# Linear attention with a gated MLP: the first v loads issued by ACT's queue, and twelve zero products fewer ahead of the first product with q

## The chip, the cores and the metric

The kernel runs on one core of one Trainium2 chip. The metric is the device time of one launch in microseconds (us), the median over runs. Engines are named as the profile names them: PE (matrix products), PEld (its weight loads), DVE, ACT and POOL (elementwise work), SP (which here only issues DMAs). ACT can issue DMAs too.

## The reference

```
kv  = einsum('bhsd,bhse->bhde', k, v)            # batch 8, heads 8, seq 576, head_dim 64
out = einsum('bhsd,bhde->bhse', q, kv)
x   = out / sqrt(mean(out*out, -1) + 1e-6) * g_norm     # heads joined: 8 x 576 x 512
h   = gelu_tanh(x @ w_in)                        # 512 -> 1024, split into u and v
v_n = (v - mean(v)) / sqrt(var(v) + 1e-6) * g_ln
v_s = einsum('ts,bsd->btd', w_sg, v_n) + b_sg[None, :, None]
y   = x + (u * v_s) @ w_out
```

## The kernel before

All eight batches run in one stream. The order of the work is written out by hand: `ORDER` is a list of words, each a step of one batch and index (`K01` is step K of batch 0, index 1), and each engine executes its instructions in the order in which the list issues them. The steps that matter here:

- `k` (load_kv, L288-296) issues the loads of one chunk of 128 tokens of k and of v; batch 0 has five (`k00` to `k04`, the last of 64 tokens), 256 KB a load for the first four and 128 KB for the last. Both go through SP's queue, k then v.
- `K` (kv, L298-313) multiplies k and v of a chunk on PE (tile `pkv`); `K04` closes batch 0. `c` (kv_high, L322-325) copies the sum out on ACT (tile `kvf`).
- `q` loads a pair of heads of q; `o` (L345-353) multiplies it with `kvf` on PE into tile `po`, eight times a batch, into the four PSUM banks "ps". `f` (o_scale) writes x from `po` with the factor g (on DVE in `f00v`), `e` (o_square) writes the squares on ACT, `s` sums them on PE.
- `N` (warm, L182-185) is two 128x512 products of a tile of zeros, whose result nobody reads. They go to the same four banks.
- `D`, `A`, `E`, `B`, `L`, `C`, `F`, `I` load a piece of w_in, w_out or w_sg and turn it from 64-bit words into two floats: A on ACT (L233), E, B and L on DVE (L241, L237, L245), C on POOL (L248), F on ACT (L259), I on POOL or DVE (L277). `F21` makes the factor g on DVE (L269).

`constants()` runs ahead of the list. Its ACT part is one small gelu, which brings an ACT_TABLE_LOAD with it.

A DMA's completion is told by one of eight semaphores, DMAHW0 to DMAHW7, shared by all DMA queues and given out in turn, so that a DMA is issued only when the earlier one on its semaphore has landed.

Of the kernel before, what the change touches and what calls it, by code (L numbers as in the profile page):

```python
# [19 lines left out]
NC = S // P  # L20
# [25 lines left out]
    t05 N31 j00 c10 j01 N32 c11 D17 j02 A04 o10 j03 j04 o11 e10 B04 k21 N33 A05 E04 N34 j05 e11 N35 B05 f10a T00 s10
    E05 f11a o12 D07 T01 T02 o13 D23 f12a T03 M04 T04 M06 e12 M02 f13v D20 M07 e13 o14 x07v o15 L05 e14 M01 F16 s11
    f14v C05 x01v e15 o16 f15v F17 M00 I16p s12 x06v f16a K20 x00v e16 I17v X00 o17 D18 M05 Y00p x02v M03 D19 f17a
    D08 x05v e17 N36 D09 x03v F20 s13 k22 x04v N37 t10 N38 k23 L04 X01 I21p N39 t11 N40 X02 N41 F18 N42 C04 N43 Y01v
    F19 m0 t12 F04 I19v F05 t13 q20 X03 I05v K21 t14 A06 Y02v Y03p t15 U00 k24 I18v k30 j10 h20 E06 q21 j11 I04v U02  # L50
    u00 j12 n00 A07 j13 n01 j14 U03 E07 u02 j15 B07 r10 n02 L07 K22 u03 n03 U06 C07 h21 k31 B06 c20 c21 r11 F07 U07
    d21 L06 u06 I07v C06 U01 u07 d20 A08 I20v F06 K30 l10 u01 r12 l11 l12 U04 l13 I06v m1 k32 E08 B08 A09 k33 V00
    n10 u04 L08 E09 C08 B09 F08 D10 n11 n12 L09 V01 n13 C09 I08v F09 D11 x10p x11v a00 I09p V02 b00 r13 a01 i20v p00
    i21v q22 y00 q23 K31 b01 z00 o20 k34 w00 p01 o21 e20 V03 k40 e21 a02 y01 b02 x13p z01 h22 w01 U05 p02 i22v a03
    x12p y02 q30 V04 u05 X10 X11 Y10v X12 Y11p b03 z02 K32 Y12v a04 k41 p03 X13 w02 Y13p V10 b04 A10 y03 p04 E10 z03
    V11 B10 L10 y04 C10 w03 z04 D12 F10 w04 S00 A11 I10v E11 S01 a10 g00 b10 G00 B11 H00 p10 S02 L11 J00 C11 g01 y10
    G01 F11 D13 S03 g02 I11p H01 J01 G02 A12 S04 g03 B12 G03 H02 E12 S05 H03 J02 g04 L12 G04 J03 P00 C12 H04 g05 J04
    G05 F12 D14 P01 Q00 I12v A13 S06 E13 Q01 B13 L13 C13 S07 g06 F13 D15 G06 I13v V12 A14 g07 z10 E14 G07 B14 w10
    L14 A15 U15 C14 E15 F14 B15 V13 f20a L15 I14v u15 C15 f21a a11 F15 b11 I15p P03 p11 a12 b12 P02 y11 p12 Q03 z11
    U16 Q02 H05 w11 H06 H07 J05 o22 a13 J06 o23 e22 b13 U12 u16 h23 f22v p13 J07 f23a P06 i23p y13 u12 e23 P07 q31  # L60
    Q06 y12 O06 z12 P05 Q07 z13 w12 O07 w13 P04 Q05 O05 o24 Q04 o25 e24 O04 U14 e25 h30 f24a i30p U13 u14 f25a q32
    o26 u13 o27 f26v e26 U11 h31 c30 i31p c31 d30 U17 u11 d31 f27a q33 e27 o30 u17 o31 f30v s20 h32 f31a i32p K40
    t20 e30 t21 e31 o32 k42 o33 t22 e32 f32v U10 k43 h33 f33v q40 e33 i33p t23 o34 u10 o35 e34 S10 q41 e35 t24 t25
    j20 j21 j22 S11 g10 j23 G10 j24 h40 K41 j25 H10 i40p g11 J10 S12 k44 G11 k50 r20 H11 S13 g12 q42 J11 G12 S14 H12
    g13 J12 G13 S15 H13 g14 r21 J13 G14 r22 P11 H14 g15 J14 G15 P12 Q11 l20 l21 l22 l23 S16 m2 Q12 n20 n21 n22 S17
    n23 g16 x21p x20v P10 G16 g17 X20 r23 G17 X21 Y20v P13 Y21p Q10 K42 Q13 H15 H16 J15 k51 H17 J16 J17 P17 P16 Q17
    O17 x23v x22p P15 Q16 O16 X22 P14 Q15 f34a Y22v O15 f35a X23 o36 Q14 o37 Y23p e36 f36v O14 V20 h41 f37v c40 i41p
    c41 d40 e37 d41 q43 s30 a20 b20 K50 t30 p20 U26 k52 t31 t32 y20 k53 t33 z20 V21 t34 u26 w20 t35 j30 j31 j32 j33
    V22 a21 j34 j35 b21 r30 p21 V23 y21 a22 z21 b22 r31 w21 p22 r32 K51 a23 y22 U23 b23 z22 k54 k60 w22 p23 U21 l30
    u23 l31 l32 l33 y23 m3 U22 z23 n30 n31 n32 x30p u21 w23 o40 u22 o41 e40 x31p U25 h42 f40v e41 n33 f41a V24 r33  # L70
    i42v u25 q50 o42 a24 o43 f42a K52 b24 h43 U20 k61 f43v p24 e42 e43 i43p y24 o44 u20 o45 e44 U24 x33p e45 q51
    x32v h50 z24 U27 i50v u24 w24 S20 q52 u27 X30 X31 Y30v S21 X32 g20 X33 Y31v G20 S22 g21 Y32p H20 J20 S23 Y33p
    g22 G22 V30 g23 G21 G23 H21 H22 J21 H23 J22 S24 a30 J23 b30 p30 P21 g24 G24 y30 P23 H24 Q21 J24 P20 Q23 S25 Q20
    V31 g25 G25 P22 a31 b31 S26 Q22 H25 p31 J25 y31 S27 g26 G26 H26 V32 g27 z30 J26 G27 z31 w30 H27 J27 P27 w31 a32
    b32 U35 Q27 p32 O27 y32 P26 z32 u35 w32 f44a U36 Q26 f45a O26 U32 u36 o46 u32 P24 f46v e46 U31 Q24 O24 P25 u31
    o47 Q25 U33 h51 f47v O25 c50 i51v c51 U37 e47 d50 q53 u33 d51 o50 u37 o51 f50a s40 f51v h52 K60 t40 e50 i52v e51
    o52 t41 q60 o53 t42 k62 f52a t43 V33 t44 f53a k63 t45 h53 j40 j41 e52 i53p j42 e53 o54 a33 o55 q61 j43 U34 e54
    b33 h60 j44 p33 e55 j45 U30 r40 u34 i60p y33 K61 u30 z33 k64 w33 S30 k70 r41 S31 g30 G30 r42 H30 S32 g31 q62 J30
    G31 S33 H31 g32 J31 G32 l40 S34 H32 l41 l42 l43 g33 m4 J32 G33 S35 n40 H33 x40v n41 X40 x41v K62 Y40p n42 X41
    r43 S36 k71 Y41v S37 n43 g34 J33 G34 g35 P31 g36 G35 H34 J34 G36 g37 P33 Q31 G37 x43v P32 x42v Q33 X42 P30 X43  # L80
    Q32 Y42p Y43p V40 Q30 H35 H36 J35 H37 J36 J37 P34 a40 b40 P35 Q34 p40 O34 y40 P36 z40 Q35 O35 w40 f54a f55v U41
    Q36 O36 o56 u41 o57 f56v e56 P37 h61 f57a i61v c60 U47 Q37 c61 e57 d60 O37 d61 q63 s50 u47 K70 t50 t51 t52 U46
    t53 k72 t54 t55 k73 j50 j51 U43 u46 j52 j53 j54 j55 V41 u43 r50 K71 r51 a41 b41 V42 r52 p41 k74 y41 z41 V43 a42
    l50 l51 l52 l53 w41 m5 b42 U40 n50 p42 a43 n51 n52 n53 x50p b43 V44 u40 x51v p43 y42 r53 z42 y43 w42 z43 K72 a44
    w43 U45 b44 U42 p44 u45 y44 z44 o60 o61 x53p U44 f60a w44 h62 x52p u42 S40 u44 i62v X50 X51 S41 Y50p X52 Y51v
    q70 e60 e61 f61a S42 Y52p X53 g40 g41 S43 g42 Y53p G42 V50 G40 G41 H40 J40 H41 g43 V51 H42 J41 a50 G43 J42 H43
    b50 o62 J43 a51 p50 P41 f62v e62 b51 P43 y50 p51 Q41 y51 P40 Q43 P42 Q40 o63 Q42 o64 f63a S44 h63 e63 i63v e64
    S45 q71 g44 G44 H44 o65 g45 S46 e65 J44 G45 h70 i70p H45 S47 J45 q72 g46 V52 G46 g47 z50 z51 w50 G47 H46 w51 H47
    U55 J46 a52 J47 b52 P46 u55 p52 y52 P45 Q46 z52 O46 w52 U56 Q45 O45 f64v P47 u56 f65v o66 Q47 U51 e66 O47 f66a
    P44 u51 U52 Q44 O44 V53 u52 o67 a53 U57 f67a b53 h71 p53 U53 c70 u57 d70 i71p c71 y53 e67 s60 u53 q73 d71 z53  # L90
    U54 t60 w53 t61 o70 t62 u54 t63 o71 f70a t64 U50 t65 h72 j60 j61 f71a i72v e70 S50 u50 j62 e71 j63 j64 j65 o72
    r60 g50 o73 f72a S51 G50 f73v h73 H50 i73v e72 J50 S52 e73 r61 g51 G51 r62 o74 H51 g52 o75 e74 J51 S53 G52 e75
    H52 l60 l61 J52 S54 l62 l63 g53 m6 G53 S55 n60 H53 g54 x60p x61v S56 G54 X60 J53 r63 X61 Y60p H54 P51 g55 J54
    Y61p P52 g56 Q51 n61 G56 n62 P53 G55 Q52 n63 S57 x63v x62p Q53 P50 X62 g57 G57 X63 Y62p Y63v V60 H55 H56 Q50 H57
    J55 J56 J57 P55 a60 b60 P54 Q55 p60 O55 y60 P56 z60 Q54 O54 w60 f74a P57 Q56 f75a O56 o76 Q57 o77 e76 f76v O57
    U66 f77a e77 s70 u66 U61 t70 t71 t72 t73 t74 U65 t75 u61 j70 j71 j72 U63 j73 u65 j74 j75 r70 V61 u63 r71 V62 a61
    r72 b61 p61 V63 y61 a62 l70 z61 l71 l72 l73 w61 m7 b62 U60 a63 n70 p62 n71 n72 n73 x70p b63 V64 u60 y62 x71p z62
    w62 U67 p63 r73 a64 b64 U62 y63 u67 p64 z63 y64 U64 u62 w63 z64 u64 w64 S60 X70 x72p X71 x73v S61 X72 Y70v Y71p
    X73 S62 g60 g61 G60 G61 H60 S63 g62 Y72p H61 Y73v V70 G62 J60 H62 J61 J62 V71 g63 a70 G63 b70 H63 p70 J63 P61
# [573 lines left out]
```

## Time and profile before

| | us |
|---|---|
| median of 3 runs | 529.02 (528.95 to 529.67) |
| the profiled execution, its own time | 528.13 |
| its span (first to last instruction) | 526.3 |
| PE busy in the span | 516.1 (98%) |

The profile is of one execution. Its span is 1.83 us shorter than its own time, which is launch and end. Times in the views count from the span's start.

### The profile page before, as it was taken

How to read it: one execution, taken by the hardware profiler on the slowest of the kernel's cores; microseconds unless marked ns; L12 is line 12 of the kernel's file. 1: busy time of each engine (PE TensorE's matmuls, PEld its weight loads, DVE VectorE, ACT ScalarE, POOL GpSimd, SP SyncE). 2: the span in 40 equal slices, each digit the busy share in tenths (PEclk: the TensorE clock that was granted, in tenths of full speed). 3: DMA queues.
4: the chain of work that ended last, by engine and by line, in shares of the span. 5: the costliest groups of instructions: out<-in, count | busy, mean ns of one | idle time of the engine just before them, and what ended most of it. 6: DMA issues, size and time to landing. Idle time of an engine off the chain costs nothing.

```text
span 526.3 us, 10121 instructions
## 1 busy us (share of the span) xinstructions
PE 516.1 (98%) x4032; PEld 476.2 (90%) x4032; DVE 313.5 (60%) x656; ACT 200.4 (38%) x449; POOL 189.3 (36%) x215
## 2 busy tenths in 40 slices
...
GB/s 249 371 277 263 209 225 152 42 42 52 108 209 94 169 158 149 24 1 45 109 205 102 68 143 100 22 24 68 47 74 45 91 57 40 2 1 91 0 24 69
DMA packets 33723, 55.51 MB, mean 105 GB/s; under 512 B 7308, under 2 KB 9228, under 8 KB 33676
## 3 DMA queue, kind: packets, MB, share of 16 engines
...
q8 instruction: 32, 0.52, 0.4%
q14 instruction: 15, 0.12, 0.1%
...
## 4 chain that ended last, share of the span: by engine, by line
PE 95%; DMA 2%; POOL 1%; ACT 1%; DVE 0%; SPq 0%; issue 0%; POOLq 0%
PE pu L540 20%; PE pg L554 19%; PE py L586 19%; PE pv L489 18%; PE po L353 5%; PE pkv L305 4%; PE warm L185 4%; PE pg L557 3%; PE pss L375 2%; DMA kv_first<-in_vx 1%; DMA v<-in_vx 1%; POOL xo L458 1%; DVE x L367 0%; SPq L296 0%; ACT sq L357 0%
## 5 line engine op out<-in xcount | busy, mean ns | idle before, releaser
L586 PE MATMUL py<-g,woh 128*128 128x288 f32 x512 | 106.6, 296 | 0.0
L567 POOL TENSOR_TENSOR gt<-gt,u 128x288 f32<-128x288 f32 x64 | 56.4, 887 | 88.4 <-DVE gt L562 79.7
L586 PEld LDWEIGHTS py<-g,woh 128*128 128x128 f32 x512 | 83.7, 188 | 0.3
L554 PE MATMUL pg<-wsh,vh 128*128 128x288 f32 x256 | 75.8, 296 | 0.0
L554 PE MATMUL pg<-wso,vh 128*128 128x288 f32 x256 | 75.6, 295 | 0.0
L586 PE MATMUL py<-g,woo 128*128 128x288 f32 x256 | 75.5, 295 | 0.0
L554 PE MATMUL pg<-wsh,vo 128*128 128x288 f32 x256 | 75.5, 295 | 0.0
L504 POOL TENSOR_SCALAR rs<-mv 128x1 f32<-128x1 f32 x36 | 12.3, 343 | 126.0 <-DVE mv L500 125.3
L574 ACT CAST g<-gt 128x288 fp32r<-128x288 f32 x64 | 27.1, 432 | 79.8 <-POOL gt L567 77.5
L562 DVE SCALAR_TENSOR_TENSOR gt<-pg,glt,b_bc 128x288 f32<-128x288 f32 x64 | 32.8, 515 | 38.2 <-PE pg L557 37.7
L591 DVE SCALAR_TENSOR_TENSOR x<-py,x 128x288 f32<-128x288 f32 x64 | 29.2, 457 | 43.9 <-PE py L586 43.1
L545 ACT ACTIVATE u<-pu 128x288 f32<-128x288 f32 x64 | 26.3, 411 | 62.8 <-PE pu L540 62.3
L586 PEld LDWEIGHTS py<-g,woo 128*128 128x128 f32 x256 | 48.2, 188 | 0.2
L554 PEld LDWEIGHTS pg<-wsh,vh 128*128 128x128 f32 x256 | 48.1, 188 | 0.3
L554 PEld LDWEIGHTS pg<-wso,vh 128*128 128x128 f32 x256 | 48.1, 188 | 0.1
L554 PEld LDWEIGHTS pg<-wsh,vo 128*128 128x128 f32 x256 | 48.2, 188 | 0.0
L540 PE MATMUL pu<-xh,wuh 128*128 128x288 f32 x256 | 45.9, 301 | 0.0
L540 PE MATMUL pu<-xh,wuo 128*128 128x288 f32 x256 | 44.3, 295 | 0.0
L540 PE MATMUL pu<-xo,wuh 128*128 128x288 f32 x256 | 44.3, 295 | 0.0
L499 DVE BATCH_NORM_STATS2 st<-hv 128x6 f32<-128x512 f32 x32 | 22.2, 693 | 33.6 <-ACT hv L494 33.4
L578 DVE TENSOR_TENSOR g<-gt,g 128x288 fp32r<-128x288 f32 x64 | 36.7, 588 | 9.0 <-ACT g L574 9.0
L540 PEld LDWEIGHTS pu<-xh,wuh 128*128 128x128 f32 x256 | 38.1, 190 | 1.6 <-issue 0.5
...
## 6 DMA issues: line engine op xcount, KB each, us to landing
...
bc<-rd SPq DMA_DIRECT2D x28, 256.0 KB, 4.0
k<-in_kx SPq DMA_DIRECT2D x24, 256.0 KB, 4.4
v<-in_vx SPq DMA_DIRECT2D x24, 256.0 KB, 4.5
kv_first<-in_kx SPq DMA_DIRECT2D x8, 256.0 KB, 5.7
kv_first<-in_vx SPq DMA_DIRECT2D x8, 256.0 KB, 6.1
...
```

Source lines behind the costliest of these rows:

```text
L353: nc.tensor.matmul(ps[:, :HS], a, m[:, t], start=(i == 0), stop=(i == len(terms) - 1))
L489: nc.tensor.matmul(pv, a[cc], w[:, cc, :], start=(n == 0), stop=(n == 11))
L499: ve.bn_stats(st, hv_[b, c])
L540: nc.tensor.matmul(pu[:, :HS], w[:, cc, f], a[b, cc][:, t], start=(i == 0), stop=(i == 11))
L545: ac.activation(u_[b, n], part["u", b, n][:, :HS], AF.Gelu_apprx_tanh, scale=W_UP)
L554: nc.tensor.matmul(ps[:, :HS], a[:, d], w[:, c, t], start=(i == 0), stop=False)
L562: ve.scalar_tensor_tensor(g_[b, n], ps[:, :HS], glt[:, dc : dc + 1], b_bc[:, half(n // 4)], op0=ALU.mult, op1=ALU.add)
L567: po.tensor_tensor(g_[b, n], g_[b, n], u_[b, n], op=ALU.mult)
L574: ac.copy(gs_[b, n][0], g_[b, n])
L578: ve.tensor_tensor(lo, g_[b, n], f32(hi), op=ALU.subtract)
L586: nc.tensor.matmul(ps[:, :HS], w[:, dc, block(n % 4)], a, start=(i == 0), stop=(i == 11))
L591: ve.scalar_tensor_tensor(xs, y_[b, n][:, :HS], W_UP, xs, op0=ALU.mult, op1=ALU.add)
```

## The change

v of batch 0 is issued by ACT in place of SP, and the words N18 to N23 are taken out of `ORDER` ("..." marks the lines that only move):

```diff
@@ ORDER
-    K04 q02 F22 N11 c00 N12 c01 N13 q03 A00 N14 N15 E00 N16 B00 q10 A01 N17 L00 N18 E01 C00 N19 q11 B01 N20 N21 N22
-    D24 F00 N23 L01 k10 I00p o00 F21 o01 k11 f00v ...
+    K04 q02 F22 N11 c00 N12 c01 N13 q03 A00 N14 N15 E00 N16 B00 q10 A01 N17 L00 E01 C00 q11 B01 D24 F00 L01 k10 I00p
+    o00 F21 o01 k11 f00v ...
...
@@ load_kv
-        for t, whole, last in ((k_[b, c], kx, kl), (v_[b, c], vx, vl)):
-            sy.dma_start(t, whole[b, :, c, :] if c < NC else last[b])
+        for t, whole, last, e in ((k_[b, c], kx, kl, sy), (v_[b, c], vx, vl, ac if b == 0 else sy)):
+            e.dma_start(t, whole[b, :, c, :] if c < NC else last[b])
```

The changed list is one line shorter, so every line number behind it is lower by one. On SP, the first DMAs of the program, before (kv_first and k, v are tiles of the first batch, ext and words pieces of weights):

```order
L296 DMA kv_first<-in_kx 128x512
L296 DMA kv_first<-in_vx 128x512
L296 DMA kv_first<-in_kx 128x512
L296 DMA kv_first<-in_vx 128x512
L296 DMA k<-in_kl 64x512
L296 DMA v<-in_vl 64x512
L216 DMA ext<-in_ex 128x513
L205 DMA words<-in_wu 128x2x512 x4
L334 DMA q<-in_qT 128x576
```

Four pairs of kv_first stand there in all, of which two are shown. On SP, the same place now:

```order
L295 DMA kv_first<-in_kx 128x512 x4
L295 DMA k<-in_kl 64x512
L215 DMA ext<-in_ex 128x513
L204 DMA words<-in_wu 128x2x512 x4
L333 DMA q<-in_qT 128x576
```

On ACT, the start of the program now, with the waits (DVE's for a constant, DMAHW1 the load of the second k, DMAHW3 that of the first v):

```order
L173 ACT_TABLE_LOAD
L173 ACTIVATE g_66<-mhalf 128x1 [waits DVE_49]
L295 DMA kv_first<-in_vx 128x512 x3
L295 DMA kv_first<-in_vx 128x512 [waits DMAHW1_49]
L295 DMA v<-in_vl 64x512 [waits DMAHW3_49]
L271 CAST heads<-ext 128x512 [waits DMAHW0_49]
```

The five loads of v have left SP and stand on ACT behind the table load and the gelu. On PE, from the fourth chunk of batch 0 to its first products with q, before:

```order
L305 MATMUL pkv<-kv_first 64x64 x8
L185 MATMUL warm<-kvh 128x512 x6
L305 MATMUL pkv<-v,k 64x64 x8
L185 MATMUL warm<-kvh 128x512 x26
L353 MATMUL po<-q,kvf 128x288 x4
L375 MATMUL pss<-sq,ones 32x144 x4
```

And the same stretch of PE now:

```order
L304 MATMUL pkv<-kv_first 64x64 x8
L184 MATMUL warm<-kvh 128x512 x6
L304 MATMUL pkv<-v,k 64x64 x8
L184 MATMUL warm<-kvh 128x512 x14
L352 MATMUL po<-q,kvf 128x288 x4
L374 MATMUL pss<-sq,ones 32x144 x4
```

Twelve of the 26 zero products between K04 and o00 are gone; nothing else on PE has moved. (A 64x64 product in these rows is two instructions in the trace, as is a 128x288 one with q.)

## Rows read from the trace of the kernel before

**Rows 1.** The page's chain that ended last, share of the span by line.

```profile
PE pu L540 20%; PE pg L554 19%; PE py L586 19%; PE pv L489 18%; PE po L353 5%; PE pkv L305 4%; PE warm L185 4%; PE pg L557 3%; PE pss L375 2%; DMA kv_first<-in_vx 1%; DMA v<-in_vx 1%; POOL xo L458 1%; DVE x L367 0%; SPq L296 0%; ACT sq L357 0%
```

**Rows 2.** Chain that ended last, 0 to 60 us: start us, us, what.

```profile
2.10 5.39 DMA kv_first<-in_vx
...
16.90 6.12 PE warm L185 x26
...
23.54 0.53 DVE x L367
...
50.53 4.85 DMA v<-in_vx
```

**Rows 3.** Timeline of PE: start us, us, what, [idle before <-what ended it].

```profile
4.77 1.12 PE L305 MATMUL pkv<-kv_first 128*64 128x64 f32 x16 [0.88 <-DMA kv_first<-in_vx]
...
7.62 1.12 PE L305 MATMUL pkv<-kv_first 128*64 128x64 f32 x16 [0.58 <-DMA kv_first<-in_vx]
...
11.74 2.35 PE L185 MATMUL warm<-kvh 128*128 128x512 f32 x6
...
14.63 1.66 PE L185 MATMUL warm<-kvh 128*128 128x512 f32 x6
```

**Rows 4.** Timeline of all engines, 16.8 to 24.5 us, and of ACT behind it.

```profile
17.01 0.74 ACT L325 COPY kvf<-pkv 64x256 f32<-64x256 f32 x2 [3.75 <-PE pkv L305]
17.78 1.24 ACT L233 ACTIVATE w<-words 128x512 f32<-128x512 f32 x2
...
18.48 0.43 DVE L241 TENSOR_SCALAR w<-w 128x512 int32<-128x512 int32 x1 [16.72 <-ACT w L233]
...
22.08 1.29 POOL L277 TENSOR_TENSOR wuo<-w,wuh 128x512 fp32r<-128x512 f32 x1 [0.74 <-ACT wuh L259]
22.15 0.14 DVE L269 TENSOR_SCALAR g<-gnt 128x1 f32<-128x1 f32 x1
...
23.34 1.28 POOL L248 TENSOR_TENSOR w<-w,words 128x512 int32<-128x512 int32 x1
23.54 0.52 DVE L367 TENSOR_SCALAR x<-po,g 128x288 f32<-128x288 f32 x1 [1.25 <-PE po L353]
```

```profile
24.69 0.69 ACT L233 ACTIVATE w<-words 128x512 f32<-128x512 f32 x1
...
26.12 0.61 ACT L259 CAST wuh<-w 128x512 fp32r<-128x512 f32 x1
```

**Rows 5.** Waits of SP's queue, 17 to 20.2 us, and of PE, 27.6 to 51.

```profile
SPq L296 <- DMA q<-in_qT: 1.8, 1, 1.8
```

```profile
PE po L353 <- ACT sq L357: 0.5, 1, 0.5
```

**Rows 6.** Timelines of SP and ACT at the start, and the first v load's time to landing.

```profile
1.16 0.42 SPq L296 DMA_DIRECT2D kv_first<-in_vx  x1
```

```profile
0.72 1.28 ACT L174 ACT_TABLE_LOAD   x1 [0.72 <-PEq L624]
2.02 0.20 ACT L174 ACTIVATE g<-mhalf 128x1 f32<-128x1 f32 x1
```

```profile
kv_first<-in_vx SPq DMA_DIRECT2D x1, 256.0 KB, 3.5
```

**Rows 7.** Busy time by stretch; the last two columns are DMA share and GB/s.

```profile
0.00:2.00 2.00, 0.19 (x1) 0.19 (x2) 0.72 (x7) 1.28 (x1) 1.47 (x7) 1.00 0.12 24
2.00:4.00 2.00, 1.89 (x4) 0.98 (x4) 0.00 (x0) 0.21 (x2) 0.68 (x2) 1.00 0.85 285
4.00:6.00 2.00, 1.23 (x17) 1.14 (x18) 0.00 (x0) 0.00 (x0) 0.00 (x0) 1.00 0.75 216
6.00:8.00 2.00, 1.42 (x9) 0.73 (x11) 0.00 (x0) 0.00 (x0) 0.00 (x0) 1.00 0.90 302
```

**Rows 8.** PE at 54 us: timeline, and the stretch behind it (granted clock third from the end).

```profile
54.22 1.12 PE L305 MATMUL pkv<-v,k 128*64 128x64 f32 x16 [2.60 <-DMA v<-in_vx]
```

```profile
54.20:57.60 3.40, 3.20 (x36) 2.94 (x37) 3.40 (x7) 1.34 (x2) 1.41 (x1) 0.50 0.58 188
```

More of the change, by code (lines that the diff above doesn't have):

```diff
@@ L41 @@
     k00 k01 k02 k03 N00 k04 N01 K00 D22 N02 D00 K01 D01 N03 N04 D02 K02 N05 D03 N06 N07 q00 K03 N08 D21 N09 N10 q01
-    K04 q02 F22 N11 c00 N12 c01 N13 q03 A00 N14 N15 E00 N16 B00 q10 A01 N17 L00 N18 E01 C00 N19 q11 B01 N20 N21 N22
-    D24 F00 N23 L01 k10 I00p o00 F21 o01 k11 f00v e00 o02 e01 f01v C01 o03 A02 f02v k12 s00 e02 B02 o04 F01 E02 o05
-    f03a f04v I01p o06 k13 e03 f05v e04 L02 o07 e05 s01 f06a f07v C02 s02 A03 k14 N24 e06 E03 N25 F02 B03 K10 D04
-    e07 I02p L03 N26 D05 K11 D06 s03 N27 t00 k20 C03 K12 t01 N28 N29 q12 F03 t02 t03 K13 q13 I03v N30 t04 D16 K14
@@ L46 @@
[L46 to L99, printed above, removed]
-    y70 a71 b71 P63 Q61 p71 y71 P62 Q63 P60 Q62 S64 Q60 S65 g64 G64 H64 S66 g65 J64 G65 S67 H65 g66 J65 G66 U76 H66
@@ L101 @@
-    g67 z70 J66 G67 z71 w70 U75 u76 H67 w71 J67 P65 u75 P66 Q65 O65 P67 Q66 O66 U77 Q67 O67 P64 u77 U72 Q64 O64 V72
-    u72 V73 a72 b72 p72 U70 y72 a73 z72 b73 U71 w72 u70 p73 U74 y73 u71 z73 w73 S70 u74 S71 g70 G70 H70 S72 g71 J70
-    G71 U73 H71 g72 J71 G72 S73 u73 H72 J72 S74 g73 G73 H73 S75 g74 J73 G74 P71 H74 g75 J74 G75 P73 Q71 H75 O71 J75
-    S76 Q73 O73 S77 g76 G76 H76 P70 g77 J76 G77 P72 Q70 H77 O70 J77 P74 Q72 O72 P75 Q74 O74 P76 Q75 O75 P77 Q76 O76
-    Q77 O77
+    K04 q02 F22 N11 c00 N12 c01 N13 q03 A00 N14 N15 E00 N16 B00 q10 A01 N17 L00 E01 C00 q11 B01 D24 F00 L01 k10 I00p
@@ new lines @@
+    o00 F21 o01 k11 f00v e00 o02 e01 f01v C01 o03 A02 f02v k12 s00 e02 B02 o04 F01 E02 o05 f03a f04v I01p o06 k13
+    e03 f05v e04 L02 o07 e05 s01 f06a f07v C02 s02 A03 k14 N24 e06 E03 N25 F02 B03 K10 D04 e07 I02p L03 N26 D05 K11
+    D06 s03 N27 t00 k20 C03 K12 t01 N28 N29 q12 F03 t02 t03 K13 q13 I03v N30 t04 D16 K14 t05 N31 j00 c10 j01 N32 c11
+    D17 j02 A04 o10 j03 j04 o11 e10 B04 k21 N33 A05 E04 N34 j05 e11 N35 B05 f10a T00 s10 E05 f11a o12 D07 T01 T02
+    o13 D23 f12a T03 M04 T04 M06 e12 M02 f13v D20 M07 e13 o14 x07v o15 L05 e14 M01 F16 s11 f14v C05 x01v e15 o16
@@ new lines @@
+    f15v F17 M00 I16p s12 x06v f16a K20 x00v e16 I17v X00 o17 D18 M05 Y00p x02v M03 D19 f17a D08 x05v e17 N36 D09
+    x03v F20 s13 k22 x04v N37 t10 N38 k23 L04 X01 I21p N39 t11 N40 X02 N41 F18 N42 C04 N43 Y01v F19 m0 t12 F04 I19v
+    F05 t13 q20 X03 I05v K21 t14 A06 Y02v Y03p t15 U00 k24 I18v k30 j10 h20 E06 q21 j11 I04v U02 u00 j12 n00 A07 j13
+    n01 j14 U03 E07 u02 j15 B07 r10 n02 L07 K22 u03 n03 U06 C07 h21 k31 B06 c20 c21 r11 F07 U07 d21 L06 u06 I07v C06
+    U01 u07 d20 A08 I20v F06 K30 l10 u01 r12 l11 l12 U04 l13 I06v m1 k32 E08 B08 A09 k33 V00 n10 u04 L08 E09 C08 B09
@@ new lines @@
+    F08 D10 n11 n12 L09 V01 n13 C09 I08v F09 D11 x10p x11v a00 I09p V02 b00 r13 a01 i20v p00 i21v q22 y00 q23 K31
+    b01 z00 o20 k34 w00 p01 o21 e20 V03 k40 e21 a02 y01 b02 x13p z01 h22 w01 U05 p02 i22v a03 x12p y02 q30 V04 u05
+    X10 X11 Y10v X12 Y11p b03 z02 K32 Y12v a04 k41 p03 X13 w02 Y13p V10 b04 A10 y03 p04 E10 z03 V11 B10 L10 y04 C10
+    w03 z04 D12 F10 w04 S00 A11 I10v E11 S01 a10 g00 b10 G00 B11 H00 p10 S02 L11 J00 C11 g01 y10 G01 F11 D13 S03 g02
+    I11p H01 J01 G02 A12 S04 g03 B12 G03 H02 E12 S05 H03 J02 g04 L12 G04 J03 P00 C12 H04 g05 J04 G05 F12 D14 P01 Q00
@@ new lines @@
+    I12v A13 S06 E13 Q01 B13 L13 C13 S07 g06 F13 D15 G06 I13v V12 A14 g07 z10 E14 G07 B14 w10 L14 A15 U15 C14 E15
+    F14 B15 V13 f20a L15 I14v u15 C15 f21a a11 F15 b11 I15p P03 p11 a12 b12 P02 y11 p12 Q03 z11 U16 Q02 H05 w11 H06
+    H07 J05 o22 a13 J06 o23 e22 b13 U12 u16 h23 f22v p13 J07 f23a P06 i23p y13 u12 e23 P07 q31 Q06 y12 O06 z12 P05
+    Q07 z13 w12 O07 w13 P04 Q05 O05 o24 Q04 o25 e24 O04 U14 e25 h30 f24a i30p U13 u14 f25a q32 o26 u13 o27 f26v e26
+    U11 h31 c30 i31p c31 d30 U17 u11 d31 f27a q33 e27 o30 u17 o31 f30v s20 h32 f31a i32p K40 t20 e30 t21 e31 o32 k42
@@ new lines @@
+    o33 t22 e32 f32v U10 k43 h33 f33v q40 e33 i33p t23 o34 u10 o35 e34 S10 q41 e35 t24 t25 j20 j21 j22 S11 g10 j23
+    G10 j24 h40 K41 j25 H10 i40p g11 J10 S12 k44 G11 k50 r20 H11 S13 g12 q42 J11 G12 S14 H12 g13 J12 G13 S15 H13 g14
+    r21 J13 G14 r22 P11 H14 g15 J14 G15 P12 Q11 l20 l21 l22 l23 S16 m2 Q12 n20 n21 n22 S17 n23 g16 x21p x20v P10 G16
+    g17 X20 r23 G17 X21 Y20v P13 Y21p Q10 K42 Q13 H15 H16 J15 k51 H17 J16 J17 P17 P16 Q17 O17 x23v x22p P15 Q16 O16
+    X22 P14 Q15 f34a Y22v O15 f35a X23 o36 Q14 o37 Y23p e36 f36v O14 V20 h41 f37v c40 i41p c41 d40 e37 d41 q43 s30
@@ new lines @@
+    a20 b20 K50 t30 p20 U26 k52 t31 t32 y20 k53 t33 z20 V21 t34 u26 w20 t35 j30 j31 j32 j33 V22 a21 j34 j35 b21 r30
+    p21 V23 y21 a22 z21 b22 r31 w21 p22 r32 K51 a23 y22 U23 b23 z22 k54 k60 w22 p23 U21 l30 u23 l31 l32 l33 y23 m3
+    U22 z23 n30 n31 n32 x30p u21 w23 o40 u22 o41 e40 x31p U25 h42 f40v e41 n33 f41a V24 r33 i42v u25 q50 o42 a24 o43
+    f42a K52 b24 h43 U20 k61 f43v p24 e42 e43 i43p y24 o44 u20 o45 e44 U24 x33p e45 q51 x32v h50 z24 U27 i50v u24
+    w24 S20 q52 u27 X30 X31 Y30v S21 X32 g20 X33 Y31v G20 S22 g21 Y32p H20 J20 S23 Y33p g22 G22 V30 g23 G21 G23 H21
@@ new lines @@
+    H22 J21 H23 J22 S24 a30 J23 b30 p30 P21 g24 G24 y30 P23 H24 Q21 J24 P20 Q23 S25 Q20 V31 g25 G25 P22 a31 b31 S26
+    Q22 H25 p31 J25 y31 S27 g26 G26 H26 V32 g27 z30 J26 G27 z31 w30 H27 J27 P27 w31 a32 b32 U35 Q27 p32 O27 y32 P26
+    z32 u35 w32 f44a U36 Q26 f45a O26 U32 u36 o46 u32 P24 f46v e46 U31 Q24 O24 P25 u31 o47 Q25 U33 h51 f47v O25 c50
+    i51v c51 U37 e47 d50 q53 u33 d51 o50 u37 o51 f50a s40 f51v h52 K60 t40 e50 i52v e51 o52 t41 q60 o53 t42 k62 f52a
+    t43 V33 t44 f53a k63 t45 h53 j40 j41 e52 i53p j42 e53 o54 a33 o55 q61 j43 U34 e54 b33 h60 j44 p33 e55 j45 U30
@@ new lines @@
+    r40 u34 i60p y33 K61 u30 z33 k64 w33 S30 k70 r41 S31 g30 G30 r42 H30 S32 g31 q62 J30 G31 S33 H31 g32 J31 G32 l40
+    S34 H32 l41 l42 l43 g33 m4 J32 G33 S35 n40 H33 x40v n41 X40 x41v K62 Y40p n42 X41 r43 S36 k71 Y41v S37 n43 g34
+    J33 G34 g35 P31 g36 G35 H34 J34 G36 g37 P33 Q31 G37 x43v P32 x42v Q33 X42 P30 X43 Q32 Y42p Y43p V40 Q30 H35 H36
+    J35 H37 J36 J37 P34 a40 b40 P35 Q34 p40 O34 y40 P36 z40 Q35 O35 w40 f54a f55v U41 Q36 O36 o56 u41 o57 f56v e56
+    P37 h61 f57a i61v c60 U47 Q37 c61 e57 d60 O37 d61 q63 s50 u47 K70 t50 t51 t52 U46 t53 k72 t54 t55 k73 j50 j51
@@ new lines @@
+    U43 u46 j52 j53 j54 j55 V41 u43 r50 K71 r51 a41 b41 V42 r52 p41 k74 y41 z41 V43 a42 l50 l51 l52 l53 w41 m5 b42
+    U40 n50 p42 a43 n51 n52 n53 x50p b43 V44 u40 x51v p43 y42 r53 z42 y43 w42 z43 K72 a44 w43 U45 b44 U42 p44 u45
+    y44 z44 o60 o61 x53p U44 f60a w44 h62 x52p u42 S40 u44 i62v X50 X51 S41 Y50p X52 Y51v q70 e60 e61 f61a S42 Y52p
+    X53 g40 g41 S43 g42 Y53p G42 V50 G40 G41 H40 J40 H41 g43 V51 H42 J41 a50 G43 J42 H43 b50 o62 J43 a51 p50 P41
+    f62v e62 b51 P43 y50 p51 Q41 y51 P40 Q43 P42 Q40 o63 Q42 o64 f63a S44 h63 e63 i63v e64 S45 q71 g44 G44 H44 o65
```

17 lines of the change are left out of this document (added).

## Prediction

> **What bounds the kernel now.** I read the page first, then the chain of waits, then the timelines of the first 30 us. Nearly the whole chain is PE, and the zero products (warm) are 4% of it, about 21 us: they cost as much as real work where they stand on it [rows 1]. The change touches only the first 28 us. There the chain runs: the second v load, issued at 2.10 and landed at 7.49 (2.10 + 5.39); then PE without a break up to 16.90; then 26 zero products in 6.12 us; then the first product with q and its scaling on DVE at 23.54 [rows 2]. The reader is to see two things. The 26 zero products stand between K04, which ends at 16.90, and o00, so they set the start of o00. And PE has stood still twice before them, for 0.88 us ahead of K00 and 0.58 us ahead of K01, both for a v [rows 3].
>
> **Part one: twelve zero products go.** One takes 6.12 / 26 = 0.235 us [rows 2], twelve 2.82 us. The 14 left end at 16.90 + 14 x 0.235 = 20.2, so o00 could begin there and not at 23.0. It also needs q: SP's wait for a q load ended with its issue at about 20.15 (1.8 us of waiting in the stretch that ends at 20.2), so the first q is there at that time [rows 5]. It needs kvf, copied from 17.01 on and done when ACT goes on at 17.78 [rows 4]. So PE gets its 2.8 us.
>
> What comes behind does not. f00v, which scales o00's result, runs on DVE with the factor g, and g is made at 22.15, ended at 22.29 [rows 4]. DVE gets there from 18.48 on through six conversions of words in a row; they began when ACT had done its first word scaling, at 17.78 behind the kvf copies, which wait for K04. This string hangs on K04 and not on the zero products. DVE then stood for 1.25 us until o00 was there, at 23.54 [rows 4]. With o00 early, f00v begins about 22.31: of the 2.82 us of PE time, 1.23 us reach the chain and 1.6 us become idle time of PE behind o03, when the four banks are full.
>
> Is something else late next? The squares of o02 stand on ACT behind a word scaling that needs a buffer POOL frees at 22.08 + 1.29 = 23.37, and the following conversion needs POOL's addition, done at 23.34 + 1.28 = 24.62 [rows 4]. With everything from f00v on 1.23 us earlier, ACT comes to them at 24.69 - 1.23 = 23.46 and 26.12 - 1.23 = 24.89 [rows 4]: both just fit, so there is no room for a larger gain here. From 27.6 us on PE runs to 51 with no wait but 0.5 us for squares [rows 5], through the loads of batch 1 too: none of them is late by the trace, and SP's next free issue waits for conversions that come earlier by as much. I cost the rest as a plain shift, up to the wait for v of batch 2 at 50.53 to 55.38 [rows 2], whose issue hangs on the same conversions. If loads that fill the queues do not move up with them, part of the 1.23 us is given back there; I leave that in the range.
>
> **Part two: v on ACT's queue.** ACT begins with a table load, 0.72 to 2.00, and a gelu that ends at 2.22. The first v was issued by SP at 1.16 and landed 3.5 us later [rows 6]. On ACT it is issued at about 2.22, 1.06 us later. At the same 3.5 us it lands at 5.7, K00 begins at 5.83, and K01 cannot begin before the time K00 and the two zero products behind it take: 7.62 - 0.58 - 4.77 = 2.27 us [rows 3], so at 8.1 against 7.62. That is 0.5 us late.
>
> K01 also needs the second v. By the bytes [rows 7], the core moved 0.57 MB from 2 to 4 us, 0.43 from 4 to 6 and 0.60 from 6 to 8, with 0.05 ahead of them, so 0.62, 1.05 and 1.65 MB up to 4, 6 and 8. SP's first load goes out at about 0.7, one issue of 0.42 us ahead of the 1.16 [rows 6], and up to 2 us only 0.05 MB moved, so its data begin near 1.8, 1.1 us behind the issue (an estimate from these rows). ACT's begin by that near 3.3 us, at some 0.42 MB. If the 16 engines then serve both queues alike, two v (0.52 MB) are done with 0.52 MB of SP's, at 1.46 MB: 7.4 us. Before, the second v was the fourth load, 1.05 MB, reached at 6.0 us, and landed at 7.49, 1.5 us behind its bytes. So 7.4 to 8.9, K01 at 7.5 to 9.0; the middle is 0.6 us late, and with the 0.5 of the first v I take 0.5. From below: if both queues together fill the idle 15, 25 and 10% of the DMA engines [rows 7] and v lands in less than 3.5 us, K01 could begin up to 0.6 us earlier, at 7.0. From above: if SP's five k (1.18 MB) and ext (0.26) all go ahead, two v are done at 1.96 MB, at the last row's 302 GB/s by 9.0 us, 10.5 with the same 1.5 us; K01 at 10.6, 3.0 us late.
>
> The Trainium skill speaks against this part (DMA: Bandwidth & Descriptors, "Issuing engines are not separate DMA queues"): DMAs from several engines run on the same 16 DMA engines and interleave, and a second issuer saves only issue time. By that rule alone there is nothing to win but SP's issue, 0.42 us a load, and the sum stands as by the middle above.
>
> From K01 to K04 PE does not wait, and the first part runs at half speed: six zero products took 2.35 us at 11.74 and 1.66 at 14.63 [rows 3]. If the clock rises at the same moment, a late K01 costs half of its delay at K04, otherwise all. Half to all of 0.5 us: I take 0.4 us. The remaining v have 2 to 4 us of products between them and cost nothing unless the bound above holds. ACT itself is idle at that time, and its five issues delay nothing there.
>
> **The sum.** The profiled execution: 528.13 - 1.23 + 0.4 = 527.3 us. It was 0.9 us faster than the median of the runs shown, 529.02. Measured against that median: 529.02 - 0.83 = 528.2 us.
>
> **Rivals.**
> 1. Two queues feed the engines better at the start. For it: DMA share of 0.75 between 4 and 6 us while loads were waiting [rows 7]. Against it: v starts a microsecond later. K01 0.6 us earlier, and since DVE's string hangs on K04 it all counts: 1.23 + 0.6 = 1.8 us, 527.2.
> 2. Slower: v comes late. It starts behind the table load and shares the engines with k, ext and words, none of which PE needs as soon. Place: K01. Price: up to 3.0 us at K04 against 1.23 won, 529.02 + 1.8 = 530.8. It decides as soon as K04 is more than 1.23 us late.
> 3. PE's new idle time drops its clock. At 54.22 PE had stood for 2.60 us, and the granted clock was 0.50 (1.2 of 2.4 GHz) for the 3.4 us behind [rows 8]. Here PE would stand some 1.3 us, from the end of o03 near 22.3 to the squares of o01 at 23.6 (f00v 0.52, then two squares in a row of 0.4 each). At half clock for 3.4 us, at most 1.7 us of work is lost: 528.2 + 1.7 = 529.9. Against it: the idle time is half as long, with products on both sides. The Trainium skill states the same mechanism (TensorE: Matmul & The Clock Gate, "Part 1"): the throttled clock is the default and activity releases it. The row at 54 us agrees.
> 4. The first q comes later than now, since SP's order now has ext and words ahead of some v and SP waits for v loads before q. At 22 us or later, nothing of part one is left: 529.4 with K04's 0.4.
>
> **How the numbers follow.** Forecast (gain 0.3 to 1.3 us, 527.7 to 528.7) 0.46, rival 1 0.25, rival 2 0.14, rival 3 0.08, rival 4 0.07. A measurement tells 0.2%, 1.06 us, from no change, so the forecast itself lies just within that. Faster, below 527.96: rival 1 with 0.24, and a third of the forecast, 0.16: 0.40. Slower, above 530.08: two thirds of rival 2, 0.10, and a little of rival 3, 0.02: 0.12. Within: 0.48. The range from 526.7 to 529.8 takes in the forecast, rival 1, most of 4 and half of 3, and leaves out most of rival 2.
>
> **What would show it.** Right: 14 zero products behind K04; K01 between 7.5 and 9.0 us; o00 about 2.4 us earlier than 23.0; DVE without idle time between g and f00v; PE idle some 1.3 us for squares ahead of the sums; the wait at 54 us as long as before but earlier. Wrong: f00v waiting for o00 as before (then q or K04 was late), K01 beyond 9.0 us, a granted clock of 0.50 between 20 and 28 us, or PE waiting for a load of batch 1.

## The result and the profile after

The changed kernel took 533.39 us, the median of 7 runs (532.15 to 536.06); the kernel before, beside it on the same chip, 529.43 (7 runs, 528.42 to 530.07). The ratio is 1.0084, with a 95% interval of 1.0063 to 1.0106: slower by 4 us where 528.2 was predicted, and outside the range. The profiled execution was the slowest of the seven, 536.06 us with a span of 534.3, 8.0 us over the span of before. So its trace shows the places of the loss, and somewhat too much of each.

Timeline of PE after the change, 4 to 62 us (start, duration, what, idle time ahead and what ended it), the lines that answer to [rows 3, 8]:

```profile
7.19 1.12 PE L304 MATMUL pkv<-kv_first 128*64 128x64 f32 x16 [3.30 <-DMA kv_first<-in_vx]
...
11.00 1.12 PE L304 MATMUL pkv<-kv_first 128*64 128x64 f32 x16 [1.53 <-DMA kv_first<-in_vx]
14.06 1.12 PE L304 MATMUL pkv<-kv_first 128*64 128x64 f32 x16
...
20.44 3.47 PE L184 MATMUL warm<-kvh 128*128 128x512 f32 x14
23.76 2.10 PE L352 MATMUL po<-q,kvf 128*128 128x288 f32 x8
...
27.02 0.74 PE L374 MATMUL pss<-sq,ones 128*32 128x144 f32 x8 [1.17 <-ACT sq L356]
...
58.74 1.12 PE L304 MATMUL pkv<-v,k 128*64 128x64 f32 x16 [4.66 <-DMA v<-in_vx]
```

K00 waits 3.30 us for the first v where it waited 0.88, K01 begins at 11.00 instead of 7.62, and the wait for v of batch 2 has grown from 2.60 to 4.66 us. Subtracting the start of the same PE instruction before from that after gives the loss as it builds up. Columns e1 and e2 are the two halves of the change by themselves, told below (us; a minus is earlier than before):

| PE instruction (start before, us) | after | e1: products only | e2: queue only |
|---|---|---|---|
| K01 (7.62) | +3.38 | -0.08 | +2.26 |
| K04 (16.22) | +3.61 | -1.60 | +0.49 |
| first sums pss (24.89) | +2.13 | -2.21 | +0.49 |
| last pss of that stage (47.80) | +2.45 | -1.46 | +0.46 |
| first pv (70.34) | +5.80 | -0.51 | +0.91 |
| py (105.50) | +7.28 | -0.49 | +0.87 |
| pv (184.56) to the last pv (483.18) | +8.0 | +0.45 | +1.33 |

Nothing is won or lost behind 185 us. In after, K04 is 3.61 us late, the sums only 2.13; 3.35 us are added between 48 and 70 us, 1.5 and 0.7 at two waits that before did not have. Waits of PE in after, 70 us to the end (what waited for what: us in total, times, longest):

```profile
PE pv L488 <- POOL xo L457: 1.6, 1, 1.6
PE po L352 <- ACT x L364: 0.4, 1, 0.4
```

The chain of waits in after, 0 to 100 us (start, duration, what), the answer to [rows 2]:

```profile
2.25 8.62 DMA kv_first<-in_vx
...
25.83 0.07 DVE g L268
26.01 0.53 DVE x L366
...
52.75 7.14 DMA v<-in_vx
```

The second v, issued at 2.25, was under way for 8.62 us against 5.39; the second v load of batch 2 for 7.14 against 4.85. Between them the chain runs through g on DVE, not through o00 and the zero products.

The start on ACT, timeline of after (ACTq is its DMA queue):

```profile
0.72 1.28 ACT L173 ACT_TABLE_LOAD   x1 [0.72 <-PEq L623]
1.82 0.39 ACTq L295 DMA_DIRECT2D kv_first<-in_vx  x1
2.01 0.20 ACT L173 ACTIVATE g<-mhalf 128x1 f32<-128x1 f32 x1
2.25 2.82 ACTq L295 DMA_DIRECT2D kv_first<-in_vx  x3
```

and the stretches of after, to be held against [rows 7, 8] (granted clock, DMA share and GB/s at the end):

```profile
2.00:4.00 2.00, 1.89 (x4) 0.97 (x4) 0.00 (x0) 0.20 (x2) 0.69 (x2) 1.00 0.83 251
4.00:6.00 2.00, 0.00 (x0) 0.00 (x0) 0.00 (x0) 0.00 (x0) 0.00 (x0) 1.00 0.97 314
...
58.20:64.90 6.70, 6.00 (x48) 5.75 (x49) 3.91 (x13) 1.21 (x3) 0.00 (x0) 0.50 0.54 143
```

v left at 1.82, earlier than the 2.22 I had counted, and yet the first one landed 5.2 us later, at 7.06. From 4 to 6 us the DMA engines were busier than before (0.97 against 0.75) and moved more (314 against 216 GB/s), and PE did nothing at all. Whose bytes they were, the DMA queues of after tell (q1 is SP's, q10 ACT's; packets, MB, share of the 16 engines). From 0 to 4.2 us SP's queue alone moved data:

```profile
q1 hardware_dynamic: 327, 0.61, 47.1%
```

From 4.2 to 8.4 us the two moved nearly the same:

```profile
q1 hardware_dynamic: 287, 0.51, 52.4%
q10 hardware_dynamic: 300, 0.56, 37.4%
```

The first packet of a v is in the trace at 4.22 us, 2.4 us behind its issue; SP's first is at 1.76, 1.04 us behind the issue at 0.72. And behind the wait at 54 us the clock stood at 0.50, the 1.2 GHz level, for 6.7 us instead of 3.4.

The column of the granted clock does not tell of the program's start: it stands at 1.00 in the rows of before from 0 to 8 us [rows 7], though the sixteen products of K00 and of K01 take 1.12 us there and those of K03, at 14.01, 0.69. At the start the level is read from the lengths of the products.

### The profile page after: what moved, and what is told of

It is laid out like the page before. It is cut to its first block, busy times and chain, and to the rows that moved or that the text cites. A ratio compares the mean times of both kernels' runs of the same rounds, so it can differ in the third digit from the quotient of the medians.

```text
span 534.3 us, 10098 instructions
## 1 busy us (share of the span) xinstructions
PE 515.6 (97%) x4020; PEld 475.5 (89%) x4020; DVE 313.9 (59%) x656; ACT 200.7 (38%) x449; POOL 189.9 (36%) x215
## 4 chain that ended last, share of the span: by engine, by line
PE 92%; DMA 4%; DVE 1%; ACT 1%; POOL 0%; issue 0%; SPq 0%; ACTq 0%; DVEq 0%
PE pu L539 20%; PE pg L553 19%; PE pv L488 18%; PE py L585 18%; PE po L352 5%; PE pkv L304 4%; PE pg L556 3%; PE warm L184 3%; PE pss L374 2%; DMA kv_first<-in_vx 2%; DMA v<-in_vx 1%; DMA out_y<-x 1%; DVE words L236 0%; DVE x L366 0%; POOL xo L457 0%
```

## The experiments

All kernels compute the whole result; only zero products, queues and the order of issues differ. Each ratio is against runs of the kernel before, beside it on the same chip.

**e1: the products alone.** The order of after, all loads on SP as before.

```diff
@@ load_kv, against after
-        for t, whole, last, e in (... (v_[b, c], vx, vl, ac if b == 0 else sy)):
-            e.dma_start(...)
+        for t, whole, last in (... (v_[b, c], vx, vl)):
+            sy.dma_start(...)
```

> The twelve zero products left out, all loads on SP as before. Theory (the loss came whole from the queue, and DVE's string of word conversions lets 1.2 us of the 2.8 us through): K01 starts near 7.6 us, K04 ends near 16.9, the scaling on DVE starts about 22.3, PE stands some 1.2 us ahead of the first sums, and the time is 0.8 to 1.5 us under before. Rival (the missing products themselves cost, by a clock that falls or by loads that come too late behind them): a granted clock of 0.50 between 18 and 30 us or a longer wait of PE at 54 us, and a time equal to before or above.

530.80 us (12 runs) against 528.71: 1.0039 [1.0018, 1.0061], slower, where part one alone had 1.23 us to win. Timeline of PE in e1 (columns as above):

```profile
20.57 2.18 PE L352 MATMUL po<-q,kvf 128*128 128x288 f32 x8 [1.87 <-DMA q<-in_qT]
...
53.50 1.02 PE L304 MATMUL pkv<-v,k 128*64 128x64 f32 x16 [3.10 <-DMA v<-in_vx]
```

o00 waited 1.87 us for the first q. PE was 1.60 us ahead at K04, where nothing is changed (K02's products already took 0.69 us in this run, 1.12 before), and 2.2 at the sums, so the twelve products themselves brought 0.6 us there. It was 1.5 us ahead at 48 us and 0.5 us at 70; between them it waited 3.10 us instead of 2.60. At 177 us PE waited for ACT's x, and the rest was gone (+0.45). This was one of the fastest of the 12 runs (528.54, the median is 2.3 higher), so where the median's loss lay it could not show. The mean granted clock of the runs hinted at it: one stretch of 3.4 us at half clock takes 3.4 x 0.5 / 526 = 0.3% off the mean, two 0.65%. Nine of the 12 runs of e1 had 0.994 or less, and all seven of after; of the 28 of before beside e1, 6. Over the runs it was 0.9937 for e1 and 0.9963 for before.

**e2: the queue alone.** v of batch 0 on ACT, the order of before with all 26 products.

```diff
@@ load_kv, against before
-        for t, whole, last in ((k_[b, c], kx, kl), (v_[b, c], vx, vl)):
+        for t, whole, last, e in ((k_[b, c], kx, kl, sy), (v_[b, c], vx, vl, ac if b == 0 else sy)):
```

> v of batch 0 on ACT's queue, all 26 zero products kept. Theory (v late on ACT's queue): K01 starts near 11 us, K04 some 3.6 us late, the first product with q too, and since nothing is won in between the time is 3 to 6 us above before, about 1.2 us worse than the change at the same point of the chain. Rival (queue and products together do the harm): K04 late as much, but the whole time at or under that of the change.

530.89 us (11 runs): 1.0051 [1.0026, 1.0075]. K00 waits for its v:

```profile
7.67 1.12 PE L305 MATMUL pkv<-kv_first 128*64 128x64 f32 x16 [3.79 <-DMA kv_first<-in_vx]
...
12.30 0.69 PE L305 MATMUL pkv<-kv_first 128*64 128x64 f32 x16
```

K01 was 2.26 us late. In the traced run (529.98) only 0.49 of that was left at K04: K02's sixteen products, the next line of e2, already took 0.69 us, as in e1's run, while before and in after they took 1.12 as the line of after shows, and only K03's took 0.69. Then 0.4 more was lost at 54 us and 0.45 at 177: 1.3 us in this trace, of the 2.2 between the medians; where the rest lies in the other runs no trace shows. The two halves together make 2.1 + 2.2 us by the medians (2.1 + 2.7 by the ratios), about the 4.0 measured: each half costs, and nearly the same.

**e3: the queue mended.** After, with ACT's table load and gelu behind the first v issues.

```diff
@@ constants
-        ac.activation(g8, mhalf, AF.Gelu_apprx_tanh)
@@ load_kv, behind the loop over k and v
+        if (b, c) == (0, 2):
+            ac.activation(g8, mhalf, AF.Gelu_apprx_tanh)
```

> As the change, but ACT issues its first three v loads ahead of the table load and the small gelu, so at 0.7 us and not at 1.8. Theory A (the late start lets SP's k loads run ahead on the 16 DMA engines): the first v lands under 5.5 us, K01 starts at 7.0 to 8.2, and the time is 0.5 to 1.5 us under before. Theory B (sharing the engines with a second queue is what costs, whenever v starts): K01 still starts at 9.5 us or later, and the time stays over before by 1 us or more.

529.51 us (12 runs): 1.0016 [0.9995, 1.0037]. Timeline of PE in e3:

```profile
4.92 1.12 PE L305 MATMUL pkv<-kv_first 128*64 128x64 f32 x16 [1.04 <-DMA kv_first<-in_vx]
...
20.78 2.18 PE L353 MATMUL po<-q,kvf 128*128 128x288 f32 x8 [2.08 <-DMA q<-in_qT]
```

Started a microsecond earlier, v comes in time, and K01 (7.13) waits for nothing. That gives back 0.7 of after's 0.8%. What is left against e6 below, which has the same start and all 26 products, is the products' part; in this trace o00 waits 2.08 us for q, and PE 3.64 us at 54 us.

**e4: are ext and words in v's way?** After, with ext (and what stands behind it on SP) held until v's second load has landed.

```diff
@@ before the load of ext
+            ac.copy(part["ext"][:, :1], v_[0, 1][:, :1])
```

> As the change, but SP's load of ext, and with it all that SP issues behind it, waits for the second v to have landed (a one-column copy from v into ext's tile by ACT). Only the k loads then share the engines with v ahead of K01. If ext and the first words in SP's queue delayed v: K01 starts 1 us or more under 11.0, at 8.5 to 10. If the k loads alone and the late start did it: K01 at 10.5 or later. In both cases the words and q come later by what was held, 1 to 3 us, so the whole time may be above that of the change.

532.74 us (6 runs): 1.0070 [1.0043, 1.0096].

```profile
9.70 1.12 PE L305 MATMUL pkv<-kv_first 128*64 128x64 f32 x16 [5.81 <-DMA kv_first<-in_vx]
```

With no ext or words on the engines, the first v landed even later (9.56). So the weights are not needed to make v late; only k loads went with it. Why it landed 2.5 us later than in after, the trace does not show.

**e5: all 26 products out,** v on SP.

```diff
-    ... N11 c00 N12 c01 N13 q03 A00 N14 N15 E00 N16 B00 q10 A01 N17 L00 N18 ... N23 ...
+    ... c00 c01 q03 A00 E00 B00 q10 A01 L00 ...
```

> All 26 zero products between K04 and the first product with q left out, all loads on SP. Theory (from the clocks that each run lists: without the products PE's clock stands at half for longer, and the first product waits for q or for DVE's string anyhow): nothing more is won, the mean granted clock is at or under 0.994 in most runs, and the time is 1 to 4 us above before. Rival (PE's products are the bound and the twelve were too few): the time falls under before by up to 3 us.

532.00 us (10 runs): 1.0052 [1.0025, 1.0079]. PE waited 3.42 us for q, and the clock fell twice. Stretches of e5:

```profile
21.60:24.90 3.30, 3.30 (x8) 2.15 (x7) 2.41 (x5) 1.51 (x4) 2.57 (x3) 0.50 1.01 351
55.80:62.50 6.70, 6.36 (x49) 6.11 (x50) 3.85 (x12) 1.57 (x3) 0.00 (x0) 0.50 0.58 159
```

The zero products ahead of o00 keep the clock up while q is on its way. With fourteen of them no stretch there is at half in the traces of after and e1; with none one is.

**e6: e3's start with all 26 products.** The order of before, v of batch 0 on ACT's queue, and e3's edit.

> v of batch 0 on ACT's queue, its first three loads ahead of the table load, and all 26 zero products kept. If the table load ahead of v made the queue lose, and the missing products the rest: first v landed by 5 us, mean clock like before's (0.996), time from 1.5 us under before to equal. If a second queue is worth nothing even when it starts in time, or costs by sharing: 0 to 1.5 us above before.

528.09 us (12 runs) against 529.66: 0.9967 [0.9945, 0.9989], faster. K00 at 5.09, K01 at 7.29 without a wait. The same queue move that costs 0.5% in e2 gains 0.3% when it starts in time. Its mean clock was 0.9962 and that of before beside it 0.9944, so some 0.2 of the 0.3% is clock; K01 itself came 0.33 us earlier than before.

**e7: a second trace of e1.**

> The products alone again, for a second trace, as the first was one of its fast runs with a clock of 0.997. If it shows 0.993 or 0.994: theory A, a second stretch of half clock lies between 18 and 30 us, where the products were; theory B, it lies at the wait near 54 us, where the clock comes back one stretch later (6.8 us at half in place of 3.4).

530.35 us, one run. o00 at 21.41 after 1.65 us for q, the wait at 54 us 3.17; one stretch at half clock, as in e1's trace, with a mean clock of 0.996. So neither theory was decided here.

**e8: e1 with six zero products in PE's idle time behind o03,** written to the banks tagged "po", which batch 0 does not use.

```diff
-    ... e00 o02 e01 f01v C01 o03 A02 ...
+    ... e00 o02 e01 f01v C01 o03 N18 N19 N20 A02 ...
-        ps = PS("warm")
+        ps = PS("warm", "po" if 18 <= 10 * i + j < 24 else "ps")
```

> The twelve products left out as in the run of the products alone, and six zero products put behind the fourth product with q, into the idle time of PE ahead of the first sums (into two free PSUM banks). If that idle time is what takes the clock: mean clock back at 0.996 in most runs and the time 1 to 2 us under that of the products alone (530.8). If the second stretch of half clock lies elsewhere, at the wait for v of batch 2 near 54 us: clocks stay at 0.993 to 0.994 in most runs and the time stays within 0.7 us of 530.8.

527.84 us (10 runs): 0.9981 [0.9960, 1.0002], 0.6% below e1. In its traced run the wait at 54 us was 3.5 us, and the clock stayed at half for two stretches behind it:

```profile
53.40:60.10 6.70, 6.40 (x49) 6.15 (x50) 4.63 (x13) 1.64 (x4) 0.61 (x1) 0.50 0.61 194
```

So six products here do not always cure what happens at 54 us. But this run was one of the slower ones: six of the ten had a mean clock of 0.996 or 0.997, where three of e1's 12 did, and the time fell by more than either forecast allowed. Over the runs e8 had 0.9946 and before beside it 0.9944; e1 had 0.9937 and before beside it 0.9963. Against their own before that is 0.28% between them, 1.5 of the 3 us; by the two means alone, taken on different chips, 0.5 us. Where the rest comes from, and why filling PE's idle time at 22 us helps the clock at 54, is not shown.

**e9: the wait at 54 us filled.** e6 with ten zero products ahead of v of batch 2.

```diff
-    ... X03 I05v K21 t14 ...
+    ... X03 I05v N44 N45 N46 N47 N48 K21 t14 ...
```

> v of batch 0 on ACT's queue ahead of the table load, all 26 zero products kept, and ten more zero products (2.35 us) ahead of the product with v of batch 2, into PE's wait near 54 us. If the half clock behind that wait comes from PE's idle time there: no granted clock of 0.50 between 50 and 65 us in most runs, mean clock 0.999 to 1.000, and 1 to 2 us under the same kernel without them (528.1). If the clock falls anyhow or the products come in the way of v: same time as without them, or above by up to 1 us.

525.88 us (11 runs) against 529.15: 0.9949 [0.9933, 0.9966]. Stretches of e9 about 54 us:

```profile
50.00:54.00 4.00, 2.48 (x24) 1.71 (x23) 3.70 (x6) 2.39 (x4) 1.74 (x2) 1.00 0.89 279
54.00:58.00 4.00, 3.91 (x41) 3.87 (x42) 4.00 (x14) 1.65 (x3) 0.00 (x0) 1.00 0.66 191
```

No half clock is left there, and every run's mean was 0.999 or 1.000. This is the lowest median measured here, 3.3 us under before; the intervals of e12 and e13 overlap with it.

**e10: e3 and e8 together** (v first, 14 products, six behind o03).

> The change with both mends: v's first three loads ahead of the table load, the twelve zero products left out ahead of the first product with q, and six put behind the fourth product, into PE's idle time. If the mends add up: mean clock 0.996 in most runs, and 0.5 to 1.5 us under the kernel with v first and the 26 products kept (528.1). If the first q, which lands near 20 to 21 us whatever PE does, sets the start of the products with q: the same time as that kernel within 0.7 us, with PE waiting for q.

527.28 us (11 runs): 0.9963 [0.9947, 0.9979]. o00 stood at 20.06 after 1.16 us of idle time; against e6 (0.9967) the products' removal brings nothing, even with the idle time filled.

**e11: is it the head start?** e2, with SP's first k held until ACT's table load is over, so that both queues start late, ACT's at 1.82 and SP's at 2.32.

```diff
@@ load_kv, ahead of the loop over k and v
+        if (b, c) == (0, 0):
+            ac.copy(k_[b, c][:, :1], mhalf)
```

> As the queue alone (all products kept, v on ACT behind the table load), but SP's first k load waits for ACT's gelu too, so that both queues start together, some 1.6 us late. Theory A (v is late since the k loads, issued ahead of it, run ahead on the 16 DMA engines): the first v lands 5 us or less behind its issue, K00 starts at 6.3 to 7.2 and K01 without a long wait, the time is 0 to 1.5 us under the queue alone (530.9). Theory B (v on ACT behind a table load is slow whatever SP does): K00 starts at 7.2 or later as in the queue alone, and everything behind it is as late or later.

529.66 us (10 runs) against 529.15: 1.0030 [1.0011, 1.0049]; the ratio to before is 0.2% better than e2's 1.0051, with intervals that overlap. The trace is what decides here:

```profile
6.79 1.12 PE L307 MATMUL pkv<-kv_first 128*64 128x64 f32 x16 [2.90 <-DMA kv_first<-in_kx]
```

K00 now waits for k. The first v, issued at 1.82 as in after, landed at 4.39: 2.6 us of way instead of 5.2, with k behind it instead of ahead, and K01 began at 9.00 without a wait. The same issue on the same queue takes twice as long when SP's k loads are ahead of it.

**e12: all mends,** e10 with e9's ten products.

> v first on ACT, twelve zero products left out ahead of the first product with q, six put behind the fourth, and ten put into PE's wait near 54 us. If the mends add: mean clock 0.999 to 1.000 and 0.5 to 1.5 us under the kernel that keeps the 26 products and fills the wait (525.9). If the wait for v of batch 2 then takes back what PE gained, since that load does not come earlier by as much: within 0.5 us of 525.9.

526.37 us (11 runs) against 528.73: 0.9960 [0.9936, 0.9985]. No better than e9.

**e13: the decisive one for the products.** e1 with e9's ten products, nothing else.

> The products alone (twelve left out, all loads on SP), with ten zero products put into PE's wait near 54 us. Theory A (the further half clock lies at that wait): clocks at 0.999 to 1.000 in most runs, and 3 us or more under the products alone (530.8). Theory B (it lies ahead of it, where the twelve products were): clocks at 0.996 to 0.997 in most runs, 1 to 2.5 us under 530.8.

526.71 us (10 runs): 0.9953 [0.9931, 0.9975], 0.86% or 4.5 us below e1's ratio. All ten runs had a mean clock of 0.999 or 1.000, where e1 had 0.9937. The stretch behind 54 us in e13, and its waits of PE over the whole run:

```profile
54.00:58.00 4.00, 3.31 (x48) 3.15 (x48) 4.00 (x8) 1.70 (x4) 1.41 (x1) 1.00 0.74 210
```

```profile
PE pkv L305 <- DMA kv_first<-in_vx: 1.7, 3, 0.7
PE po L353 <- POOL w L248: 1.1, 1, 1.1
PE po L353 <- DMA q<-in_qT: 1.0, 1, 1.0
```

e1's half clock lay at the wait at 54 us, and nowhere else behind the start: filling that one wait takes all of it away. By the mean clocks it is 0.57% of 526 us, 3 of the 4.5 us. The same ten products gave e6 only 1.0 us (e9, with intervals that overlap), so most of what they give e1 is a loss of its own. The kernel before with these ten products and nothing else was not run; it has one such stretch in its own trace, worth up to 1.7 us.

## Why the prediction was wrong, point by point

**Held: DVE's string.** f00v was forecast to follow g without idle time and not to wait for o00. Timeline of DVE in after:

```profile
25.15 0.68 DVE L244 SCALAR_TENSOR_TENSOR w<-words,w 128x512 int32<-128x512 int32 x1
25.76 0.14 DVE L268 TENSOR_SCALAR g<-gnt 128x1 f32<-128x1 f32 x1
26.01 0.52 DVE L366 TENSOR_SCALAR x<-po,g 128x288 f32<-128x288 f32 x1
```

It starts 0.11 us behind g's end, with no wait shown. K04 is 3.61 us late and f00v 2.47 (26.01 against 23.54): 1.14 us won back, where 1.23 was forecast. In e8 and e13, measured from K04, the sums come 1.35 us earlier than before. PE's idle time ahead of the sums was 1.17 us, forecast 1.3, and the clock did not fall there.

**Failed: "K01 at 7.5 to 9.0", the term of 0.5 us.** It was 3.38 us late, past the bound from above of 3.0. The even sharing held: while two v were moved, 0.52 MB, SP's queue moved 0.51 MB. Two other steps failed. ACT's data were to begin 1.1 us behind the issue, as SP's do, "near 3.3 us"; they began at 4.22, 2.4 us behind an issue that was even earlier than forecast. So the bytes of two v were through at 8.34 and not at 7.4: the 0.9 us of the late beginning, at the speed that was forecast. And the second v landed 2.5 us behind its bytes, at 10.87, where 0 to 1.5 us were allowed. The first six loads landed in the order of their issues, over both queues: three k at 4.08, 4.72 and 5.57, the first v at 7.06, the fourth k at 10.20, the second v at 10.87. The bound from above, 10.6 for K01 "if SP's five k and ext all go ahead", came nearest by its number, not by its reason. e4 and e11 show what matters: k and not ext, and which of the two is issued first. So rival 2's place was right, and of its mechanism the late start and k, not ext and words; its chance of 0.14 was too small, and its price too low.

The Trainium skill's rule, which the prediction weighed (DMA: Bandwidth & Descriptors, "Issuing engines are not separate DMA queues"), is that DMAs of several issuers interleave on the same 16 engines and that a second issuer saves only issue time. The trace agrees: from 4.2 to 8.4 us both queues moved data side by side, and in e6 K01 came 0.33 us earlier, less than one issue of 0.42 us. What a late start costs does not follow from that rule: the same load took 2.6 us in e11 and 5.2 us in after.

**Failed: "half to all of it" at K04.** 3.61 us arrived of 3.38: all and a little more, since from K01 to K03 PE took 6.64 us (11.00 to 17.64) and before 6.39 (7.62 to 14.01); in e2's traced run 0.49 arrived of 2.26, less than half. Both ends of this term were too tight.

**Not safe: "So PE gets its 2.8 us".** That q was there at 20.15 was read from the moment at which SP's wait for one q load ended, with no row for its first use in an earlier place. o00 waited for q and began at 20.57 in e1, 20.78 in e3 and 21.41 in e7; in e8 it began at 19.71 without a wait. After itself hides it, K04 being so late. In e1 the sums were 0.6 us earlier than K04's shift alone makes them, where 1.23 was forecast: there K04 was 1.60 us early and q was not, so q held o00, and f00v waited 0.55 us for it.

**Failed: "a plain shift, up to the wait for v of batch 2".** In e1 PE was 2.2 us ahead at the sums and only 0.5 us at 70. I had left that in the range, as a gain given back. What I had not seen is that with PE ahead the wait there can get longer (3.10 to 3.64 us in e1, e3, e7 and e8 against 2.60; in e6 and e10 v came earlier as well and it did not), and that behind a longer wait the clock stays at half for 6.8 us more often: in none of the five traces with a wait of up to 2.6 us, in two of five with 3.1 to 3.7, in both with more than 4. Rival 3 had this mechanism, with the very row that shows it [rows 8], and looked for it at 22 us, where 14 products keep the clock up. It was at work 30 us later, at the wait that existed already. There, the second half stretch costs 3.4 / 2 = 1.7 us; by the mean clocks e1 loses 0.26% or 1.4 us more than its before, of 2.1.

**Not settled.** Why the data of the second queue begin so late, and why the second v landed 2.5 us behind its bytes, no trace says. The second v load of batch 2 took 7.14 us in after's trace against 4.85, and why is open too; the two later waits, 1.6 us for POOL's xo and 0.4 for ACT's x, each cost after something, and the one at about 177 us cost e1 and e2 0.95 and 0.45 too. The trace names the engines but no run was made on them. And half or more of e8's gain is unexplained.
